# Sixteen small GpSimd loads into scratch tiles, beside a decode kernel that streams its cache

## The chip, the cores and the metric

The kernel runs on one core of a Trainium2 chip. The metric is device time in microseconds for one execution; the time before is the median of three runs, and one execution was also taken by the hardware profiler.

## What is computed

One decode step: attention over the last 4,096 positions of a cache and a dense block with the Mish activation, both on the same normalised input, added to the input.

```python
def _A_ref(x, k_cache, v_cache, wq, wo):       # x: 2 x 1 x 448, 16 query heads, 8 kv heads, 256 wide
    W = min(4096, max(256, Sk // 4))           # Sk = 32768: the last 4096 positions
    q = (x @ wq).reshape(B, Sq, Hq, Dh)...
    k, v = the last W rows of k_cache, v_cache, each kv head for two query heads
    p = _softmax(einsum("bhqd,bhkd->bhqk", q, k) * Dh ** -0.5)
    return einsum("bhqk,bhkd->bhqd", p, v)... @ wo
def _B_ref(x, w1, b1, w2):
    h = x @ w1 + b1
    return (h * tanh(softplus(h))) @ w2
xn = _layernorm(x)
return x + _A_ref(xn, ...) + _B_ref(xn, ...)
```

All inputs are bfloat16. The windows of both caches are 2 x 8 x 4096 x 256 values each, 33.6 MB for K and as much for V; with the weights 77.67 MB are read from HBM.

## The kernel before

The work on the caches is done in four turns, `u` = 0 to 3, each for two kv heads of both batch entries (`KU * Bsz` = 4 streams). A turn's keys come in two loads of 4 MB (`load_k`, L102), its values in two more (`load_v`, L110), and its slice of Wo in one (`load_wo`, L116). All of these are issued by SP, in program order, and go through a ring of three buffers of 4 MB, `kv_pool`; Wq, and at the end W2, take a buffer of the same ring. A load waits on SP until the buffer's last reader is done, and the loads written behind it wait too. W1 is loaded at L541, the ragged rows of W2 by `load_xb` and `load_xa` (L607, L613) in turns 0 and 1, and the rest of W2 at L638 after the loop. The only load of another queue is that of x (L123, on ACT).

In a turn, `turns` (L306) transposes a key buffer on VectorE, `scores` (L382 to L404) makes the scores on TensorE, their exponentials on ScalarE and transposes these on VectorE, `weigh` sums them, `values` (L439) multiplies with V, and `gather`, `finish`, `relay` and `mix_early` (L457 to L519) bring the result through Wo. In the last turn the second value buffer comes in three parts, of which the last two go through `values_fixed` (L472), and `mix` and `dense_out` (L286) end the sum. `pace` (L658) issues matmuls whose result is not used. The tile framework is under a manual schedule: each engine's instructions stand in the order in which the code is written, and semaphores are set where one engine's data is another's input or where a buffer is used again.

GpSimd (POOL) has set-up work only: constants, masks, zeroed tiles and four copies, the last of them the memset of `w2_x` at L537. Nothing in the loop is on GpSimd, and it issues no load. `consts` is a pool with one buffer for each tile, and tiles of the pool `small` are allocated after it. At the end of the program SP waits for every semaphore in use, and all engines go through closing barriers.

The loop around the change:

Of the kernel before, what the change touches and what calls it, by code (L numbers as in the profile page):

```python
# [11 lines left out]
BF16 = mybir.dt.bfloat16  # L12
FP32 = mybir.dt.float32
# [4 lines left out]
def kernel(  # L18
# [13 lines left out]
    nc = tc.nc  # L32
# [47 lines left out]
    consts = ctx.enter_context(tc.tile_pool(name="consts", bufs=1))  # L80
# [18 lines left out]
    def load_k(u, r):  # L99
        t = ring("k")  # L100
        src = kview[u][:, s0:, :].rearrange("j (c t) d -> c j (t d)", c=C)
        nc.sync.dma_start(out=t[:], in_=src[:, :, r * RK * KE : (r + 1) * RK * KE])  # L102
        k_t[u, r] = t

    def load_v(u, g, lo=0, hi=TV):
        if lo == 0:
            v_t[u, g] = ring("v")
        t = v_t[u, g]
        src = vview[u][:, s0:, :].rearrange("j (g x t) d -> g x j (t d)", g=GV, x=C)
        nc.sync.dma_start(  # L110
            out=t[:, lo * Dh : hi * Dh], in_=src[g, :, :, lo * Dh : hi * Dh]
        )

    def load_wo(u):
        w = wo_pool.tile([P, KU, rep, 2 * D], BF16, tag="wo", name="wo")
        nc.sync.dma_start(  # L116
            out=w[:].rearrange("p k h e -> p (k h e)"),
            in_=A_wo.rearrange("(k u y i) d -> u y k (i d)", k=KU, u=U, i=8)[u],
        )
        wo_t[u] = w  # L120
# [7 lines left out]
    for lo, hi in ((0, HW // 2), (HW // 2, NS * HW // 2), (NS * HW // 2, NS * HW)):  # L128
# [14 lines left out]
        out=halves[:], in_=ident[0:2, 0:2].unsqueeze(2).to_broadcast([2, 2, Bsz])  # L143
# [5 lines left out]
    for k in range(KU):  # L149
        nc.gpsimd.tensor_copy(  # L150
            out=hot[:, k, :, :, :, k],
            in_=ident[:].rearrange("p (q y) -> p y q", y=4).unsqueeze(2)
# [11 lines left out]
        out=rstd[:], in_=mv[:, 1:2], func=ACT.Sqrt, bias=eps_t[:], scale=1.0  # L164
# [4 lines left out]
        out=xn_bf[:],  # L169
# [8 lines left out]
        out=parm[:], in_=ident[:].rearrange("p (a o) -> p o a", o=2), axis=AXIS.X, op=ALU.add  # L178
# [3 lines left out]
        out=jm[:],  # L182
        in_=ident[:].rearrange("p (a j h) -> p j a h", j=J, h=rep),
# [4 lines left out]
        out=jm[:], in0=jm[:], scalar1=-1.0, scalar2=29952.0, op0=ALU.add, op1=ALU.mult  # L188
# [3 lines left out]
        out=mneg[:], in_=jm[:].unsqueeze(1).to_broadcast([P, TH * 8, J])  # L192
    )
    sel = consts.tile([P, 2, NQ], FP32)
    for x in range(2):
        for w in range(4):
            at = 32 * w + (2 * (w % 2) + x) * NQ
# [3 lines left out]
            else:  # L201
                nc.vector.tensor_tensor(
                    out=sel[:, x, :], in0=sel[:, x, :], in1=src, op=ALU.add
# [9 lines left out]
        out=pick_f[0:QB, 0:12],  # L213
        in_=idb.rearrange("p (a s) -> p a s", s=XB),
# [4 lines left out]
        out=pick_f[QB:P, XO:XP].rearrange("p (e r) -> p e r", r=4)[:, :, 0:2],  # L219
        in_=ida.rearrange("p (e r s) -> p e r s", r=2, s=XA),  # L220
# [4 lines left out]
        out=pick_f[QB:P, XP : XP + XA],  # L225
        in_=ida.rearrange("p (a s) -> p s a", s=XA),
# [4 lines left out]
        out=pick_f[0:QB, XP:],  # L231
        in_=idb.rearrange("p (a s) -> p s a", s=XB),
# [20 lines left out]
    for odd in range(2):  # L253
        for half in range(2):
            o = (half + odd) % 2
            nc.vector.tensor_scalar(
                out=xs[:, odd::2, half * Bsz : (half + 1) * Bsz],
# [45 lines left out]
    def turns(u, i):  # L303
        t = k_t.pop((u, i))
        for r in range(RK):
            nc.vector.transpose(  # L306
                out=kt[i][:, :, r, :, :],
                in_=t[:, r * KE : (r + 1) * KE].bitcast(FP32).rearrange(
                    "p (a c j) -> p a c j", c=P // (R * J), j=J
                ),  # L310
            )

    spread = {}
    for n in range(2):
        for e in range(2):
# [3 lines left out]
                out=sp[:],  # L319
                in_=ident[:, o : o + 63 : 2].unsqueeze(1).to_broadcast([P, G, 32]),  # L320
# [56 lines left out]
    def scores(u, i):  # L377
        if i == 0:
            state["ex"] = small.tile([P, T, 4, NH, J], BF16, tag="ex", name="ex", bufs=1)
        ex = state["ex"]  # L380
        sc = ps_sc.tile([P, T, 4, J], FP32, tag="sc", name="sc")
        nc.tensor.matmul(  # L382
            sc[:].rearrange("p t c m -> p (t c m)"),
            lhsT=ident[:],
            rhs=mneg[:].rearrange("p a j -> p (a j)"),
            start=True,
            stop=False,
            skip_group_check=True,
        )
        for n in range(NB):  # L390
            for e in range(2):
                for w in range(4):
                    nc.tensor.matmul(  # L393
                        sc[32 * w : 32 * (w + 1)].rearrange("p t c m -> p t (c m)"),
                        lhsT=qd[:, u, 2 * n + e, :, :].rearrange("p g q -> p (g q)"),
                        rhs=ktm[i][:, n, e, :, 16 * w : 16 * (w + 1)],
                        start=False,
                        stop=(n == NB - 1 and e == 1),
                        skip_group_check=True,
                    )  # L400
        nc.scalar.activation(out=ex[:, :, :, i, :], in_=sc[:], func=ACT.Exp, scale=scale)  # L401
        if i == NH - 1:
            for h in range(NH):
                nc.vector.transpose(  # L404
                    out=p_all[:, :, h * TH : (h + 1) * TH, :].rearrange("p g t q -> p t g q"),
                    in_=ex[:, h * TH : (h + 1) * TH].rearrange(
                        "p t c i m -> p t (c i m)"
                    ).rearrange("p t (g q) -> p t g q", g=G),
                )
            swap()  # L410
# [20 lines left out]
    def values(u, g, hi=TV):  # L431
        if g == 0:
            state["v", u] = ps_v.tile([P, 2, Dh], FP32, tag="v", name="pv")
        pv = state["v", u]
        v = v_t[u, g]
        for k in range(hi // 2):
            a, b = k // 2, k % 2
            w = 2 * (a % 2) + b
            nc.tensor.matmul(  # L439
                pv[32 * w : 32 * (w + 1), :, :].rearrange("p x d -> p (x d)"),  # L440
                lhsT=p_run[:, g, 4 * a : 4 * a + 4, :].rearrange("p t q -> p (t q)"),
                rhs=v[:, 2 * k * Dh : (2 * k + 2) * Dh],
                start=(g == 0 and a < 2),
                stop=(g == GV - 1 and a >= hi // 4 - 2),
                skip_group_check=True,
            )
# [92 lines left out]
    def load_w1():  # L539
        t = consts.tile([P, NS * F2], BF16, name="w1")  # L540
        nc.sync.dma_start(  # L541
            out=t[:], in_=B_w1.flatten().rearrange("(p e) -> p e", p=P)
        )
        state["w1"] = t
# [60 lines left out]
    def load_xb(r):  # L605
        rows = B_w2[F2 + FR : F2 + FR + QB, :].rearrange("(e r s) d -> r e (s d)", r=4, s=XB)
        nc.sync.dma_start(  # L607
            out=w2_x[r:12:4, :], in_=rows[r]
        )

    def load_xa(r):
        rows = B_w2[F2 + FR + QB :, :].rearrange("(e r s) d -> r e (s d)", r=2, s=XA)
        nc.sync.dma_start(out=w2_x[XO + r : XP : 4, 0 : XA * D], in_=rows[r])  # L613

    def dense_x():
        for s in range(XS):
            nc.tensor.matmul(  # L617
                early[:],
                lhsT=act_x[:, s, :],
                rhs=w2_x[:, s * D : (s + 1) * D],  # L620
                start=False,
                stop=False,
            )
# [19 lines left out]
    def dense_out(part):  # L643
        k, lo, hi = w2_parts[part]
        for i in range(lo, hi):
# [2 lines left out]
                act_bf[:, i, k, :], state["w2"][:, at : at + D], stop=(k == 1 and i == NR - 1)  # L648
            )

    load_w1()
    def pace(n, key=None):
        ps = ps_sc.tile([P, T, 4, J], FP32, tag="sc", name="pace")
        for i in range(n):
            rhs = mneg[:].rearrange("p a j -> p (a j)")
            if key is not None and i == 0:
                rhs = key
            nc.tensor.matmul(  # L658
                ps[:].rearrange("p t c m -> p (t c m)"),
                lhsT=ident[:],  # L660
                rhs=rhs,
                start=True,
                stop=True,
                skip_group_check=True,
            )
# [10 lines left out]
    for u in range(U - 1):  # L676
        load_k(u + 1, 0)
        load_v(u, 0)
        load_k(u + 1, 1)
        load_v(u, 1)  # L680
        load_wo(u)
        if u == 0:
            load_xb(0)
            load_xb(1)
            load_xa(0)
        if u == 1:
            load_xb(2)
            load_xb(3)
            load_xa(1)
        turns(u + 1, 0)  # L690
        values(u, 0)
        scores(u + 1, 0)
        turns(u + 1, 1)
        if u == U - 2:
            pace(11, key=ktm[1][:, 0, 0, :, 0:16])
        values(u, 1)
        gather(u)
        finish(u)
        scores(u + 1, 1)
        relay(u)  # L700
        if u == U - 2:
            dense_x()
        mix_early(u)
        if u < U - 2:
            weigh(u + 1)
    u = U - 1
# [67 lines left out]
```

## Time and profile before

| | us |
|---|---|
| median of 3 runs (lowest, highest) | 188.63 (188.61, 188.82) |
| profiled execution, its own time | 188.59 |
| its span | 186.8 |
| busy: PE / DVE / ACT / POOL | 88.9 / 97.1 / 12.6 / 7.8 |
| HBM read | 77.67 MB, 416 GB/s over the span |

The profiled execution's time is 1.8 us longer than its span, which goes from the first to the last instruction. Its time is 0.04 us under the median. TensorE's mean granted clock was 0.76. In the page, q1 is the queue of SP's loads, q10 that of ACT's, and q8 and q14 fetch instructions. Times inside the span count from its start.

### The profile page before, as it was taken

To read this page: it belongs to the slowest core of one execution; us is meant where nothing else is said; L and a number is where in the kernel's file an instruction comes from. 1 tells how busy PE (TensorE), PEld (TensorE's weight loads), DVE (VectorE), ACT (ScalarE), POOL (GpSimd) and SP (SyncE) were. 2 spreads that over 40 slices of the span, in tenths; PEclk is the share of its full clock that TensorE was granted. 3 is DMA by queue.
4 is the path that set the end of the run, shared out by engine and by line. 5 is a ranking of instruction groups with operands and counts; after the bars stand their busy time and mean duration, and the time that the engine had idled before them with its cause. 6 is when DMAs were issued, how large, how long until landed. Compare 5 with 4: busy or idle time off the path is not lost.

```text
span 186.8 us, 1974 instructions
## 1 busy us (share of the span) xinstructions
PE 88.9 (48%) x854; PEld 38.1 (20%) x854; DVE 97.1 (52%) x100; ACT 12.6 (7%) x27; POOL 7.8 (4%) x18
## 2 busy tenths in 40 slices
PE   0057015893209300783039101881059059899694
PEld 0022002541003100241013000330022013434353
DVE  6961798974792098028940296048920593040100
ACT  3004000101000100110000100110000000210100
POOL 8800000000000000000000000000000000000000
PEclk9999999955555855599555855798556756999999
DMA  6999999999999999999999999999999999999991
GB/s 207 442 475 442 407 435 405 452 446 444 414 421 421 432 449 389 472 442 442 414 435 418 449 435 401 468 446 407 421 435 428 442 449 421 449 389 430 403 406 73
DMA packets 4523, 77.78 MB, mean 416 GB/s; under 512 B 522, under 2 KB 912, under 8 KB 1956
## 3 DMA queue, kind: packets, MB, share of 16 engines
q1 hardware_dynamic: 4512, 77.67, 97.2%
q8 instruction: 6, 0.10, 0.2%
q14 instruction: 1, 0.01, 0.0%
q10 hardware_dynamic: 4, 0.00, 0.0%
HBM read 77.67 MB, written 0.00 MB: 416 GB/s over the span
## 4 chain that ended last, share of the span: by engine, by line
DMA 73%; DVE 12%; PE 9%; issue 3%; SPq 1%; ACT 0%
DMA k<-in_A_k_cache_dram 44%; DMA v<-in_A_v_cache_dram 29%; DVE kt L306 12%; PE pv L439 3%; PE acc L286 1%; PE sc L393 1%; PE early L519 1%; PE early L617 1%; PE o L472 1%; SPq L129 1%; PE pace L658 1%; PE o L457 1%; PE ox_ps L498 0%; SPq L102 0%; ACT vs L451 0%
## 5 line engine op out<-in xcount | busy, mean ns | idle before, releaser
L306 DVE STREAM_TRANSPOSE kt<-k 128x4096 f32<-128x4096 f32 x16 | 70.1, 4417 | 31.1 <-DMA k<-in_A_k_cache_dram 31.1
L439 PE MATMUL pv<-v,p 128*32 128x512 bf16 x244 | 23.2, 546 | 55.8 <-DMA v<-in_A_v_cache_dram 55.8
L393 PE MATMUL sc<-kt,qd 128*32 128x512 bf16 x256 | 22.6, 489 | 11.2 <-DVE kt L306 11.2
L439 PEld LDWEIGHTS <-p 128*32 128x32 bf16 x244 | 8.5, 124 | 68.4 <-issue 44.9
L658 PE MATMUL pace<-mneg,ident 128*128 128x512 bf16 x42 | 12.7, 440 | 0.0
L393 PEld LDWEIGHTS <-qd 128*32 128x32 bf16 x256 | 7.7, 114 | 24.1 <-issue 19.7
L484 DVE TENSOR_TENSOR oT<-o,rec 128x16 bf16<-128x16 f32 x4 | 0.7, 175 | 21.1 <-PE o L457 17.5
L404 DVE STREAM_TRANSPOSE p<-ex 128x512 bf16<-128x512 bf16 x8 | 5.2, 690 | 10.6 <-ACT ex L401 10.6
L401 ACT ACTIVATE ex<-sc 128x512 bf16<-128x512 f32 x8 | 4.8, 597 | 85.4 <-PE sc L393 85.4
L425 DVE TENSOR_REDUCE rec<-dn 128x8 f32<-128x512 f32 x4 | 2.8, 691 | 13.3 <-PE dn L417 13.3
L658 PEld LDWEIGHTS <-ident 128*128 128x128 bf16 x43 | 4.2, 111 | 13.7 <-DVE kt L306 7.8
L248 PE MATMUL xr_ps<-ident,xrows 2*128 2x2 bf16 x7 | 1.0, 182 | 11.2 <-DVE xrows L247 11.2
L451 ACT COPY vs<-pv 128x512 f32<-128x512 f32 x4 | 2.3, 586 | 54.0 <-PE pv L439 54.0
L519 PE MATMUL early<-wo,ox 128*2 128x448 bf16 x24 | 5.0, 352 | 1.3 <-ACT ox L510 1.3
L457 PE MATMUL o<-sel,vs 128*128 128x8 f32 x32 | 4.3, 262 | 2.1 <-ACT vs L451 2.1
L457 PEld LDWEIGHTS o<-sel,vs 128*128 128x128 f32 x32 | 4.2, 196 | 4.5 <-ACT vs L451 4.4
L417 PE MATMUL dn<-p,ones 128*128 128x512 bf16 x8 | 2.8, 438 | 3.8 <-DVE p L375 3.8
L382 PE MATMUL sc<-mneg,ident 128*128 128x512 bf16 x8 | 4.1, 516 | 0.0
L658 PE MATMUL pace<-kt,ident 128*128 128x512 bf16 x1 | 0.6, 609 | 7.3 <-DVE kt L306 7.3
L561 PE MATMUL h_ps<-xs,w 128*128 128x4 bf16 x49 | 3.3, 186 | 0.9 <-DMA w<-in_B_w_dram 0.9
L191 DVE CAST mneg<-jm 128x512 bf16<-128x512 f32 x1 | 3.5, 3481 | 0.0
L328 PE MATMUL q_ps<-wq,xs 128*32 128x512 bf16 x28 | 3.2, 627 | 0.4 <-issue 0.4
(85 smaller groups left out, 58.4 us busy)
## 6 DMA issues: line engine op xcount, KB each, us to landing
k<-in_A_k_cache_dram SPq DMA_DIRECT2D x8, 4096.0 KB, 26.4
v<-in_A_v_cache_dram SPq DMA_DIRECT2D x7, 4096.0 KB, 21.2
wo<-in_A_wo_dram SPq DMA_DIRECT2D x4, 896.0 KB, 21.5
v<-in_A_v_cache_dram SPq DMA_DIRECT2D x1, 2560.0 KB
wq<-in_A_wq_dram SPq DMA_DIRECT2D x1, 1792.0 KB, 10.2
w<-in_B_w_dram SPq DMA_DIRECT2D x1, 1568.0 KB
wq<-in_A_wq_dram SPq DMA_DIRECT2D x1, 1536.0 KB, 6.3
v<-in_A_v_cache_dram SPq DMA_DIRECT2D x1, 1024.0 KB
```

The costliest lines, as they stand in the source:

```text
L191: nc.vector.tensor_copy(out=mneg[:], in_=jm[:].unsqueeze(1).to_broadcast([P, TH * 8, J]))
L306: nc.vector.transpose(out=kt[i][:, :, r, :, :], in_=t[:, r * KE : (r + 1) * KE].bitcast(FP32).rearrange("p (a c j) -> p a c j", c=P // (R ...
L328: nc.tensor.matmul(q_ps[32 * u : 32 * (u + 1), :], lhsT=xs[:, s, :], rhs=wq_t[s][:, u * 512 : (u + 1) * 512], start=(s == 0), stop=(s == N ...
L382: nc.tensor.matmul(sc[:].rearrange("p t c m -> p (t c m)"), lhsT=ident[:], rhs=mneg[:].rearrange("p a j -> p (a j)"), start=True, stop=Fal ...
L393: nc.tensor.matmul(sc[32 * w : 32 * (w + 1)].rearrange("p t c m -> p t (c m)"), lhsT=qd[:, u, 2 * n + e, :, :].rearrange("p g q -> p (g q) ...
L401: nc.scalar.activation(out=ex[:, :, :, i, :], in_=sc[:], func=ACT.Exp, scale=scale)
L404: nc.vector.transpose(out=p_all[:, :, h * TH : (h + 1) * TH, :].rearrange("p g t q -> p t g q"), in_=ex[:, h * TH : (h + 1) * TH].rearrang ...
L439: nc.tensor.matmul(pv[32 * w : 32 * (w + 1), :, :].rearrange("p x d -> p (x d)"), lhsT=p_run[:, g, 4 * a : 4 * a + 4, :].rearrange("p t q ...
L457: nc.tensor.matmul(po[:, c, :], lhsT=sb[:, x, c::2], rhs=sel[:, x, :], start=(x == 0 and c == 0), stop=(last and x == 1), skip_group_check ...
L519: nc.tensor.matmul(early[:], lhsT=ox[:, i, :], rhs=w[:, i, :], start=False, stop=(u == U - 2 and i == 7),)
L561: nc.tensor.matmul(h_ps[:, i, :, :].rearrange("p k b -> p (k b)"), lhsT=w1_v[:, s, cols], rhs=xs[:, s, 0 : 2 * Bsz], start=False, stop=(s ...
L658: nc.tensor.matmul(ps[:].rearrange("p t c m -> p (t c m)"), lhsT=ident[:], rhs=rhs, start=True, stop=True, skip_group_check=True,)
```

## The change

Two scratch tiles are added to `consts`: `marks`, 32 partitions of 64 float32, and `marks_b`, 32 partitions of 96 bfloat16. Two helpers load the first rows of Wo into them with DMAs issued by GpSimd. `mark_cast(n, w)` loads `n` rows of `w` elements and widens them to float32; `mark_split(n, w)` loads `n` rows in two pieces of `w` elements each, in bfloat16. The calls stand in the loop over turns: seven in turn 0 and nine in turn 1, with `w` going up by two from 24 to 54. Each load takes rows of its tile that no other one takes. Nothing reads the tiles.

```diff
+    marks = consts.tile([32, 64], FP32)
+    marks_b = consts.tile([32, 96], BF16)
+    row_at = [0, 0]
+
+    def mark_cast(n, w):
+        at = row_at[0] % 28
+        row_at[0] += n
+        nc.gpsimd.dma_start(out=marks[at : at + n, 0:w], in_=A_wo[0:n, 0:w])
+
+    def mark_split(n, w):
+        at = row_at[1]
+        row_at[1] += n
+        nc.gpsimd.dma_start(
+            out=marks_b[at : at + n].rearrange("p (a e) -> p a e", a=2)[:, :, 0:w],
+            in_=A_wo[0:n, :].rearrange("p (a e) -> p a e", a=2)[:, :, 0:w],
+        )
+
     load_w1()
...
             load_xb(2)
             load_xb(3)
             load_xa(1)
+        if u == 0:
+            for i in range(7):
+                mark_cast(2, 24 + 2 * i)
+        if u == 1:
+            for i in range(3):
+                mark_split(2, 38 + 2 * i)
+            mark_cast(3, 44)
+            for i in range(4):
+                mark_cast(1, 46 + 2 * i)
+            mark_cast(5, 54)
         turns(u + 1, 0)
         values(u, 0)
```

## The prediction

> **What bounds the kernel now.** I read the page's slices first, then the chain that ended last, then a table by stage, then the queue table, and last the single packet records of the trace, since the change adds packets.
>
> The slices show a DMA row of nines from the second slice to the last but one:
>
> ```profile
> DMA  6999999999999999999999999999999999999991
> GB/s 207 442 475 442 407 435 405 452 446 444 414 421 421 432 449 389 472 442 442 414 435 418 449 435 401 468 446 407 421 435 428 442 449 421 449 389 430 403 406 73
> ```
>
> The chain says that the end is reached over landings of K and V, with little else in it:
>
> ```profile
> DMA 73%; DVE 12%; PE 9%; issue 3%; SPq 1%; ACT 0%
> ```
>
> The table by stage has the 16 DMA engines at a mean share of about 1.0 in every stage, whatever VectorE and TensorE do in it. (Columns: stage, its length, busy time of PE, PEld, DVE, ACT, POOL with instructions, granted clock, DMA share, GB/s.)
>
> ```profile
> 4.00:8.00 4.00, 0.00 (x0) 0.00 (x0) 3.89 (x6) 0.00 (x0) 4.00 (x8) 1.00 0.99 420
> 8.00:12.00 4.00, 0.79 (x6) 0.60 (x6) 3.74 (x22) 0.00 (x0) 0.41 (x1) 1.00 1.04 446
> 12.00:16.00 4.00, 3.63 (x31) 1.24 (x30) 0.61 (x4) 0.00 (x0) 0.00 (x0) 1.00 1.04 451
> 80.00:100.00 20.00, 8.57 (x87) 3.27 (x86) 11.87 (x10) 0.81 (x3) 0.00 (x0) 0.72 1.01 436
> 140.00:160.00 20.00, 11.74 (x93) 4.09 (x85) 8.77 (x2) 1.18 (x2) 0.00 (x0) 0.66 1.01 436
> ```
>
> In the packet records 1,920 packets of 32,768 B take 1,213 ns each, 27.0 B/ns, so 16 engines carry 432 GB/s; 77.67 MB at that rate are 179.7 us, and the stream runs from 1.75 us (first packet of Wq) to 183.73 (last of W2). It is never empty: the shortest time between an issue on SP and the first packet of that load, once the stream runs, is 5.9 us (V issued at 57.22, first packet at 63.13), elsewhere mostly 8 to 17. So compute has some 6 us of cover everywhere but in the tail, and **what takes time on a DMA engine comes out at the end one for one**. After the V landing at 179.15 the tail is fixed: TensorE to 184.4, the output's store, closing barriers to 186.8.
>
> **What the change adds.** Sixteen DMA issues on GpSimd's queue, with 26 widened rows and 6 rows in two pieces each: 38 runs of 48 to 108 B as read. They wait for nothing (the rows of the two scratch tiles do not overlap, nobody reads them), and GpSimd has nothing after its last memset:
>
> ```profile
> 5.33 3.08 POOL L537 MEMSET w_x<- 48x3584 bf16 x1
> ```
>
> So all sixteen go out from 8.41 us on, whatever turn of the loop they are written in. An issue from GpSimd is not in the trace; the nearest rows are the one on ACT's queue, 0.52 us, and those on SP's, 0.27 to 0.8. At 0.5 to 1 us each they are out by 16 to 24 us. Only the closing drain stands behind them on that queue, so the issue time is off the path.
>
> *VectorE beside GpSimd.* VectorE has been slow next to GpSimd's memsets: the cast at L191 took 3.48 us and ended just after the memset above, and a copy of 2x4 elements at L142 took 1.91. If issues from GpSimd hold VectorE's copies the same way, some twenty small copies and casts between 8.6 and 20.3 us are late, then the first key transposes (L306, from 21.50, after 1.21 us of idle). Even if VectorE stood still until 24 us the first V load would go out 3 to 6 us late, and it has 13.4 us in hand (issued 30.30, first packet 43.71). I cost it at nothing; the cover is the backlog, and a delay beyond 5.9 us that lasted to 57 us would come out whole.
>
> *The DMA engines.* This is the term that decides. By their bytes the marks are nothing: an 80 B packet took 9 ns, an 896 B one 41, a 4 B completion packet 9. But they come from a second queue, and the trace has seven packets on engines that were streaming for the first:
>
> ```profile
> q1 hardware_dynamic: 4512, 77.67, 97.2%
> q8 instruction: 6, 0.10, 0.2%
> q14 instruction: 1, 0.01, 0.0%
> ```
>
> In the packet records six of these were followed by a 32 KB packet of q1 that took far more than its 1,213 ns: after the instruction fetches at 39.16, 61.05, 100.64, 125.86 and 163.92 (16 KB each) 1,764, 1,707, 1,711, 1,713 and 1,681, and after the 8 KB one at 44.91, 1,745. The lengthening is 468 to 551 ns, mean 507, and does not grow with the size of the fetch. It isn't given back: from the start of the fetch at 163.92 to the end of the packet behind it are 2.62 us, where line rate for both would be 1.82. So an interlude from another queue costs its engine about 0.51 us besides its own packets. For a tiny packet it may be less, down to nothing; I have no row for that.
>
> [...]
>
> How many interludes does an engine get? The nearest row is the two-row load of x (q10): two data packets and two completion packets, so two engines touched. By that row 32 rows touch an engine 32 times in all, twice each if they go round the sixteen (the row counts 2x7, 2x3, 3, 1x4, 5 add up to 32, two laps). Twice 0.51, and two or three runs and their completions of up to 41 + 9 ns: 2 x 0.56 = 1.12 us. The bounds are 2 x 0.02 = 0.04 us (no loss at the change) and sixteen interludes on some engine, 16 x 0.56 = 9.0. I take 1.12, as the long packets are the only rows of a queue change and the load of x is the only small load.
>
> *The close.* At the end SP waits for the semaphores of all loads, two to an instruction, 64 ns apart (185.14, 185.20, ...), and then for the output, landed near 185.95. Up to eight further semaphores are four instructions, 0.26 us: nothing if they stand before the output's wait, which has 0.6 us to spare, 0.26 if behind. I take 0.1, with GpSimd's own closing drain (78 ns now) in it.
>
> The scratch tiles take 256 + 192 B of a partition and move the tiles allocated after them; no row prices an address, and I take 0.
>
> **Sum.** 1.12 + 0.1 = 1.2 us on the profiled execution's 188.59 us (186.8 of span), 189.8; the median of the runs, 188.63, is 0.04 higher, so 189.8 stands for both.
>
> **Rivals.**
> 1. *Tiny packets slip in for nothing.* The lengthening comes from the fetches' size or target, and the marks cost 16 x 9 ns of completions and three runs, 0.2 us, with 0 to 0.1 at the close: 188.7 to 188.9. For it: within q1 a completion packet costs nothing that shows, since an engine's sixteen packets of two K loads from 10.92 to 30.28 us take 1,210 ns each with a completion among them. Against it: those come from the same queue. The same time results if the loads turn out not to be made.
> 2. *Every mark touches every engine, or all touch the same few.* Sixteen interludes at 0.51 to 0.56 us: 8 to 9 us, 196.7 to 197.6. For it: the loads of W2's ragged rows (3 and 4 rows) leave only some engines late, so that the engines' spread grows from 0.5 us at 10.9 to 1.8 at 117. Against it: two marks waiting together cost one change. It decides once the interludes on the worst engine pass about eight. [...]
> 3. *Faster.* Each landing waits for the latest engine, and the spread at the last Wo load is 1.77 us (first packet 172.43, last end 176.38, against 8 x 272 ns). Each 16 KB fetch costs one engine about 1.4 us (2.62 - 1.21). If the new queue moves one fetch from a late engine to an early one, the latest engine gains what parts it from the next group, about 0.5 us: 188.1. It decides only if the marks themselves cost under that. Nothing shows that a fetch's engine depends on other queues.
>
> **How the numbers follow.** The forecast, an interlude cost paid a few times per engine (189.1 to 193), has 0.45; rival 1 has 0.26, rival 2 0.15, rival 3 0.14. The limit of 0.2%, 0.38 us, is about what a measurement of this kernel can tell from no change; forecast and rival 2 are beyond it, rival 1 inside, rival 3 beyond it on the other side. Faster 0.14, same 0.26, slower 0.60. The range takes in rivals 1 and 3 (188.1) and goes up to the point of eight interludes, 8 x 0.56 = 4.5, 193.0; rival 2 is left out. The likeliest case's own range is 189.1 to 193.0.
>
> **What would show it.** Right: a new software queue with packets between 8 and 25 us, 32 KB packets of q1 near 1,700 ns there and nowhere else new, two or so to an engine; the K landing that starts L306 at 21.50 about 1 us later, and the last V landing as late. Rival 1: no lengthened packets, the last V landing within 0.2 us of 179.15. Rival 2: the first K landing 5 us or more late. The forecast fails if the marks go out later than 25 us, if DMA's share falls under 0.9 in stages other than the early ones, or if the added time lies behind 184 us.

## The result and the profile after

The change made the kernel 0.5% slower: 189.55 us (median of 7 runs, 189.31 to 190.51) against 188.63 (7 runs, 188.52 to 188.90), a ratio of 1.0056 with a 95% interval of 1.0037 to 1.0074. The profiled execution took 189.87 us, 0.3 over its median, with a span of 187.7. The span was 186.8 us before and is 187.4 in the median of the runs, and the time outside the span went from some 1.8 us to 2.17. So about 0.6 us came inside the span and 0.36 outside it. One of the four executions of experiment e12 below, 196.83 us, was in a slow state, and its row goes by the other three.

The slices of the kernel after, as before, show a DMA row of nines (one slice has an eight):

```profile
DMA  6999999999999998999999999999999999999991
```

The queue table has the new queue. Its columns are packets, MB and share of 16 engines' time:

```profile
q1 hardware_dynamic: 4512, 77.67, 97.0%
q0 software_dynamic: 512, 0.01, 0.2%
```

It has 512 packets for sixteen loads, 32 a load. One load of two rows alone (experiment e2) shows two data packets and 30 of 4 B. The records don't name the engine, but in the kernel after sixteen of these packets start between 12.48 and 13.62 us, sixteen more between 13.70 and 14.83, and each in the second group some 1.22 us after one in the first: by that a load has two packets on each of the 16 engines.

GpSimd's timeline (start, length, engine, line, operation; the idle time before it and its releaser in brackets) shows the issues:

```profile
5.61 3.08 POOL L537 MEMSET w_x<- 48x3584 bf16 x1
8.64 3.72 POOL L658 DMA_DIRECT2D marks<-in_A_wo_dram  x7
12.35 0.60 POOL L663 DMA_DIRECT2D marks_b<-in_A_wo_dram  x1
15.47 0.58 POOL L663 DMA_DIRECT2D marks_b<-in_A_wo_dram  x1 [2.52 <-DMA marks<-in_A_wo_dram]
31.27 0.52 POOL L658 DMA_DIRECT2D marks<-in_A_wo_dram  x1 [1.91 <-DMA marks_b<-in_A_wo_dram]
```

Eight go out at once, 0.52 to 0.65 us each. From the ninth on each waits for the semaphore of the load eight places earlier, which it uses again: the ninth, at 15.47 us, names the first one's, whose last update came at 15.19, and the sixteenth, at 31.27, the eighth one's, at 30.99. Landing is slow on the full stream. The sixteen took 6.6 to 18.6 us, where the load of x, issued at 0.74 us before the stream ran, had its last packet at 1.70. Two groups in the list of DMA issues (KB, median us from issue to landing):

```profile
marks<-in_A_wo_dram POOLq DMA_DIRECT2D x2, 0.2 KB, 8.9
marks_b<-in_A_wo_dram POOLq DMA_DIRECT2D x1, 0.3 KB, 18.6
```

In the packet records the starts are those of engines that pass one packet of q0, then one of q1, then the next of q0: some 1.22 us after the first where q1's packets are of 32 KB, and sixteen starts in 0.47 to 0.49 us between 31.5 and 33.4 us, where they are of 12,544 B. The marks run from 12.5 to 43.5 us.

At the early end VectorE's first key transposes show how late the K loads landed; the first two lines are of before, the last two of after:

```profile
21.50 8.77 DVE L306 STREAM_TRANSPOSE kt<-k 128x4096 f32<-128x4096 f32 x2 [1.21 <-DMA k<-in_A_k_cache_dram]
31.18 8.77 DVE L306 STREAM_TRANSPOSE kt<-k 128x4096 f32<-128x4096 f32 x2 [0.90 <-DMA k<-in_A_k_cache_dram]
```
```profile
21.98 8.77 DVE L306 STREAM_TRANSPOSE kt<-k 128x4096 f32<-128x4096 f32 x2 [2.41 <-DMA k<-in_A_k_cache_dram]
31.52 8.77 DVE L306 STREAM_TRANSPOSE kt<-k 128x4096 f32<-128x4096 f32 x2 [0.77 <-DMA k<-in_A_k_cache_dram]
```

At the late end the chain that ended last, in order of time (start, us, what), has the last V landing that the tail waits for at 179.15 before and at 167.57 + 12.39 = 179.96 after, and from there the same tail. Before, then after:

```profile
166.78 12.37 DMA v<-in_A_v_cache_dram
179.20 0.96 PE o L472 x32
184.38 0.37 DVE res L740
```
```profile
167.57 12.39 DMA v<-in_A_v_cache_dram
180.01 0.96 PE o L472 x32
185.20 0.37 DVE res L767
```

So the first K landings are 0.3 to 0.5 us later, and the last V landing 0.8 in this execution. A single landing measures the stream only roughly (experiment e1, without a load, has the last V landing at 179.41, 0.26 us later than before); the bytes that q1 has moved measure it better. Counted from 8 us on and compared with the kernel before, the kernel after is only 0.11 us behind at 31 us (at 432 GB/s), 0.55 at 46, and 0.57 at 80, 100 and 160 us. Nearly all is lost while the marks run, 0.44 us of it between 31 and 46, and none is won back. With 0.07 us more in the close (below) that is the 0.6 us of the median span.

In the packet records the marks on the engines show in two parts. The 512 packets themselves took 0.35 us for each engine (5.59 us over 16). And 73 packets of q1 between 8 and 80 us took more than their usual time, against 7 before the change; the added time is 0.42 us an engine against 0.10. The new long ones last 1,227 to 1,535 ns in place of 1,213, most of them between 34 and 40 us. Together that is 0.35 + 0.32 = 0.67 us, more than the 0.57 that the stream lost, because a packet and the next one overlap. The starts show it: in e2 the 32 KB packet starts 5 to 6 ns after the small one, which takes 9 or 25; from one small packet to the next on its engine are 1,215 ns with no lengthening, where two 32 KB packets in a row start 1,209 to 1,210 ns apart. By that a completion costs its engine some 5 ns and not the 9 of its own record, an estimate.

### The profile page after: what moved, and what is told of

It reads as the page before. It is cut to its first block, busy times and chain, and to the rows that moved or that the text cites. A ratio compares the mean times of both kernels' runs of the same rounds, so it can differ in the third digit from the quotient of the medians.

```text
span 187.7 us, 1994 instructions
## 1 busy us (share of the span) xinstructions
PE 86.0 (46%) x854; PEld 37.6 (20%) x854; DVE 96.3 (51%) x100; ACT 12.6 (7%) x27; POOL 16.6 (9%) x34
## 4 chain that ended last, share of the span: by engine, by line
DMA 53%; DVE 24%; PE 18%; ACT 2%; SPq 1%; issue 1%
DMA v<-in_A_v_cache_dram 38%; DVE kt L306 18%; DMA k<-in_A_k_cache_dram 15%; PE pv L439 5%; PE sc L393 5%; DVE p L404 2%; PE o L457 2%; PE acc L286 1%; PE dn L417 1%; DVE rec L425 1%; ACT ex L401 1%; ACT vs L451 1%; PE early L519 1%; PE early L617 1%; PE o L472 1%
## 5 line engine op out<-in xcount | busy, mean ns | idle before, releaser
L439 PE MATMUL pv<-v,p 128*32 128x512 bf16 x244 | 22.5, 533 | 57.6 <-DMA v<-in_A_v_cache_dram 57.6
L393 PE MATMUL sc<-kt,qd 128*32 128x512 bf16 x256 | 20.8, 456 | 12.1 <-DVE kt L306 12.0
L658 POOL DMA_DIRECT2D marks<-in_A_wo_dram x13 | 6.9, 535 | 10.2 <-DMA marks<-in_A_wo_dram 8.2
```

Source lines behind the costliest of these rows:

```text
L393: nc.tensor.matmul(sc[32 * w : 32 * (w + 1)].rearrange("p t c m -> p t (c m)"), lhsT=qd[:, u, 2 * n + e, :, :].rearrange("p g q -> p (g q) ...
L439: nc.tensor.matmul(pv[32 * w : 32 * (w + 1), :, :].rearrange("p x d -> p (x d)"), lhsT=p_run[:, g, 4 * a : 4 * a + 4, :].rearrange("p t q ...
L658: nc.gpsimd.dma_start(out=marks[at : at + n, 0:w], in_=A_wo[0:n, 0:w])
```

## The experiments

The theories:

- **A**: any GpSimd load adds a fixed 0.36 us outside the span, and each load costs its two small packets on every engine, 0.02 to 0.03 us.
- **B**: all of the cost grows with the number of loads.
- **C** and **G**: the long q1 packets come from loads that are cut into runs of 12 to 20 B. In the list of instructions the loads of one row of 48, 50 and 52 are 16 runs of 3 elements, 10 of 5 and 13 of 4.
- **D**: the 0.36 us outside the span comes from the length of GpSimd's program. **E**: it comes from GpSimd's loads.
- **F** and **H**: any run, or any widened run, lengthens the stream's next packet by some 70 ns.
- The prediction's own: 0.5 us for an interlude.

All twelve, with the medians of the runs. The last two columns are from the packet records of the profiled execution. "Own" is the time of the q0 packets for each engine, and "longer" the time added to q1's packets between 8 and 80 us for each engine, less the 0.10 of before. "Behind" is how far q1's bytes since 8 us are behind those of the kernel before at 80 us; the kernel after has 0.57. The kernel before, run beside them: 188.67 to 188.68 us, span 186.8 to 186.85, outside 1.79 to 1.82.

| run | us | ratio (95%) | span | outside | own + longer | behind |
|---|---|---|---|---|---|---|
| e1 no loads | 188.79 | 1.0000 (0.9988 to 1.0012) | 187.0 | 1.79 | 0 | 0.00 |
| e2 one load | 188.72 | 1.0001 (0.9992 to 1.0010) | 186.9 | 1.80 | 0.02 + 0 | 0.02 |
| e3 sixteen equal | 189.25 | 1.0033 (1.0021 to 1.0045) | 187.15 | 2.15 | 0.32 + 0.03 | 0.22 |
| e4 thirty-two equal | 189.61 | 1.0050 (1.0038 to 1.0063) | 187.5 | 2.09 | 0.65 + 0.05 | 0.44 |
| e5 sixteen cut rows | 190.34 | 1.0090 (1.0076 to 1.0103) | 188.3 | 2.05 | 0.50 + 1.17 | 1.55 |
| e6 sixteen memsets | 188.65 | 0.9998 (0.9989 to 1.0007) | 186.8 | 1.81 | 0 | 0.02 |
| e7 eight equal | 189.12 | 1.0025 (1.0014 to 1.0037) | 187.2 | 2.07 | 0.16 + 0.01 | 0.11 |
| e8 sixteen, not widened | 189.30 | 1.0041 (1.0019 to 1.0063) | 187.2 | 2.10 | 0.29 + 0 | 0.19 |
| e9 256 runs of 64 B | 189.23 | 1.0034 (1.0024 to 1.0043) | 187.2 | 2.17 | 0.32 + 0.04 | 0.24 |
| e10 the same, widened | 189.23 | 1.0033 (1.0022 to 1.0043) | 187.15 | 2.04 | 0.56 + 0.25 | 0.45 |
| e11 256 runs of 12 B, rows apart | 189.36 | 1.0032 (1.0021 to 1.0044) | 187.35 | 1.98 | 0.50 + 0.20 | 0.37 |
| e12 128 runs of 1,536 B | 191.68 | 1.0157 (1.0140 to 1.0173) | 189.7 | 2.13 | 0.64 + 2.14 | 2.73 |

**How the cost grows (e1, e2, e7, e3, e4).** The calls in turns 0 and 1 are replaced; e1 has none, e2 one, e7 eight, e4 thirty-two with a tile of 64 rows:

```diff
-            for i in range(7):
-                mark_cast(2, 24 + 2 * i)
...
+            for i in range(16):      # e3
+                mark_cast(2, 32)
```

e1: 

> The two scratch tiles stay declared, all sixteen loads are left out. Every theory that puts the cost into the loads: 188.6 us (within 0.1 of before), time outside the span 1.8 us, no q0 packets. If moved addresses carried part of the cost: up to 0.3 us more.

e2: 

> One load (2 rows of 24, widened), the other fifteen left out. Theory A (a fixed price for any GpSimd load outside the span, 0.36 us, plus some 0.03 us per load for its two packets on each engine): 189.0, outside the span 2.15, q0 with 32 packets. Theory B (all of it grows with the number of loads): 188.7, outside the span 1.8. The prediction's own mechanism (0.5 us for each interlude on an engine): 188.6 to 189.1 and a lengthened 32 KB packet on two engines.

e3: 

> Sixteen loads all of 2 rows of 32, widened, in place of the sixteen lengths. Theory A: as after, 189.4 to 189.6, outside the span 2.15, 512 packets in q0. Theory C (the lengthened 32 KB packets after 34 us come from the one-row loads that are cut into runs of 12 to 20 B): 189.2, no group of 1.25 to 1.5 us packets in the stream. Prediction's mechanism: 189.8.

e4: 

> Thirty-two loads of 2 rows of 32, widened, into a tile of 64 rows. Theory A: 0.5 us over the sixteen equal ones, 189.9 to 190.1, outside the span 2.15, 1024 packets in q0. Theory B: twice the whole cost, 190.4, outside the span 2.5. If the cost is fixed and does not depend on the number: as sixteen, 189.3.

e7: 

> Eight loads of 2 rows of 32, widened. In the span 8 x 0.02 us over before for Theory A, 187.0. Outside: 1.8 if the number of waits or instructions sets it (the eight have no waits of their own), 2.15 if the eight semaphores do. So 188.8 or 189.15.

Tiles without loads cost nothing that shows in the time, and neither does one load. The stream shows the price of a load best: one, eight, sixteen and thirty-two loads put it 0.02, 0.11, 0.22 and 0.44 us behind, 0.014 us a load, well under the packets' own time. Inside the span theory A is right in kind, and its price is too high. The spans fit only roughly: from sixteen to thirty-two loads the median grows by 0.35 us (187.1 to 187.4 against 187.4 to 187.9), but eight loads have 187.2, where A expected 187.0, about as much as sixteen, and e1 without a load has 187.0. So the median of a few spans is good to some 0.2 us here. The page of e4 has the packets doubled:

```profile
q0 software_dynamic: 1024, 0.01, 0.3%
```

Outside the span A and B are both wrong in part: one load adds nothing, eight and sixteen add about 0.3, and thirty-two no more. The step lies between one and eight loads. Nor is it constant: of e7's twelve runs nine have 1.98 to 2.18 us outside the span and three 1.73 to 1.82, and one to three runs of e3, e8, e9, e10 and e12 have the short time too. The prediction's 0.5 us for an interlude is far off for small packets: one such for each load would be 8 us, and the sixteen loads, with two packets on every engine, put the stream 0.22 us behind.

**The cut rows (e5).**

```diff
+            for i in range(16):
+                mark_cast(1, 48)     # made into 16 runs of 3 elements by the program
```

> Sixteen loads all of 1 row of 48, widened, which the program makes into 16 runs of 3 elements each. Theory C (such runs lengthen the stream's packets, 0.1 us per load on each engine, from the long packets between 32 and 44 us in the changed kernel): 1.8 us over the sixteen equal two-row loads, 191.0. Theory A (only the number of loads and their two packets per engine count): 189.3 to 189.5, no group of long packets.

It is 1.1 us over the sixteen equal loads, less than the 1.8 expected but in C's direction. In the packet records 256 runs of 12 B lengthened q1's packets by 18.7 us in all, 73 ns a run, and the stream is 1.33 us further behind than with the equal loads. VectorE's second pair of transposes is later by more than a microsecond, and starts in two pieces:

```profile
22.32 8.77 DVE L306 STREAM_TRANSPOSE kt<-k 128x4096 f32<-128x4096 f32 x2 [3.00 <-DMA k<-in_A_k_cache_dram]
32.63 4.45 DVE L306 STREAM_TRANSPOSE kt<-k 128x4096 f32<-128x4096 f32 x1 [1.54 <-DMA k<-in_A_k_cache_dram]
```

The changed kernel has 39 such runs, in three of its loads; its long packets fall after 34 us, where those loads pass. It took 189.55 against 189.25 us for the sixteen equal ones, 0.30 us, and the packet records put 0.29 us more lengthening on its engines (0.32 against 0.03). The intervals of the two ratios overlap (1.0037 to 1.0074, 1.0021 to 1.0045), so the times alone leave this part likely. The stream shows it: 0.57 us behind against 0.22, and between 31 and 46 us, where the cut loads pass, 0.44 against 0.06. Its 39 runs lengthened q1's packets by some 0.12 us each, more than e5's 73 ns; why stays open.

**What about a run makes it dear (e8 to e11).** e8 makes the tile of e3 bfloat16. e9 to e11 load 16 rows instead of two, so that there are sixteen runs in each load, 256 in all:

```diff
+        to = marks[16 * (i % 8) : 16 * (i % 8) + 16, w * (i // 8) : w * (i // 8) + w]
+        nc.gpsimd.dma_start(out=to, in_=A_wo[16 * i : 16 * i + 16, 0:w])   # w = 32, 32, 3
```

e8: 

> Sixteen loads of 2 rows of 32 without widening (the tile is bfloat16). Theory A: as with widening, 189.25 (189.1 to 189.4). If widening costs on the engines: 0.1 to 0.3 us less.

e9: 

> Sixteen loads of 16 rows of 32, not widened: one run of 64 B for each engine and load, 256 in all, where the two-row loads have 32. Theory F (each run from the second queue lengthens the stream's next packet by some 70 ns, whatever it is): 1.1 us over the sixteen two-row loads, 190.3. Theory G (only runs of 12 to 20 B do): 189.3 to 189.4. Theory H (only widened runs of any length): 189.3 to 189.4.

e10: 

> The same sixteen loads of 16 rows of 32, widened to float32 (128 B written for each run). Theory F: 190.3. Theory G: 189.4. Theory H: 190.3 or more.

e11: 

> Sixteen loads of 16 rows of 3, widened: 256 runs of 12 B, as in e5, but each from and to a row of its own. Theories F, G and H: 190.3. If the cost in e5 comes from neighbouring runs of one row that are written by different engines: 189.3 to 189.4.

All four stay within 0.11 us of e3. Widening costs nothing that these times can tell (e8 against e3, e10 against e9). In the packet records it does cost a little: a 32 KB packet behind a widened run is some 15 ns longer (e3, e10), behind an unwidened run of 64 B not at all (e8, e9), and e10's stream is 0.21 us further behind than e9's. At 70 ns H falls, and F too, since 256 unwidened runs leave the stream nearly where 32 do, 0.24 us behind against 0.19. G as it was put falls as well: e11 has as many runs of 12 B as e5, and is 1 us faster. There a run lengthened q1's packets by only some 12 ns. What differs is that e5's runs are neighbours in one row, in the source and in the target; e11's have a row of their own on both sides. Which side matters was not tried. In e10 own and longer add up to 0.81 us, while the stream was 0.45 behind and the span grew by 0.35: packets overlap (the 5 to 6 ns from start to start in e2), so the two columns are not paid in full.

**A larger interlude (e12).**

```diff
+        nc.gpsimd.dma_start(out=marks[16 * i : 16 * i + 16, :], in_=A_wq[16 * i : 16 * i + 16, 0:768])
```

> Eight loads of 16 rows of 768, not widened: 128 runs of 1,536 B. By the eight small ones' 189.1 plus 128 x 57 ns / 16 = 0.46 us for the bytes at the stream's rate: 189.6. With 70 ns of lengthening for each run 0.56 us more, 190.1. If an interlude of a KB and more costs the prediction's 0.5 us: 8 x 0.5 = 4 us more, 193.5.

It lies between the expectations: 2.6 us over the eight small loads, where the bytes explain 0.46. Each run of 1,536 B lengthened q1's packets by 0.27 us (34.3 us over 128 runs), against 15 ns or less for the small runs of e8 to e11 and 0.5 us for the instruction fetches of 8 and 16 KB. By the starts of the packets about half of the 0.27 falls on the q1 packet behind the run and half on the one behind its completion, some 0.13 us each. The loss is there at the first K landings:

```profile
23.09 8.77 DVE L306 STREAM_TRANSPOSE kt<-k 128x4096 f32<-128x4096 f32 x2 [3.97 <-DMA k<-in_A_k_cache_dram]
34.09 4.45 DVE L306 STREAM_TRANSPOSE kt<-k 128x4096 f32<-128x4096 f32 x1 [2.22 <-DMA k<-in_A_k_cache_dram]
```

**Outside the span (e6, and all runs).**

```diff
+            for i in range(16):
+                nc.gpsimd.memset(marks[:, 4 * i : 4 * i + 4], 0.0)
```

> No loads; sixteen small memsets on GpSimd in their place. Theory D (the 0.35 us outside the span is an instruction fetch at the program's end, set by the length of GpSimd's program): 189.0, outside the span 2.15. Theory E (it comes from loads of GpSimd, their queue or semaphores): 188.65, outside the span 1.8.

Sixteen more instructions on GpSimd that are not loads leave the time outside the span at 1.81 us. So the number of GpSimd's instructions doesn't set it, and E is left of the two. The waits of the ninth and later loads don't set it either, since e7's eight loads have none and mostly took the longer time. Two rivals are not excluded: a load may be longer in the program than a memset, and eight loads also bring eight semaphores that SP waits for at the end (107 to 114 in the kernel after). In the packet records a sign goes with the longer time. In eight of the profiled executions (the changed kernel, e4, e5, e8 to e12) there is an instruction fetch of 8 KB on q14 some 1.8 to 2 us after the span's end, and all of these have 2.06 to 2.25 us outside the span. In the six others (before, e1, e2, e3, e6, e7) there is none, and they have 1.74 to 1.85. The profiled executions of e3 and e7 are among the few of theirs with the short time. So the 0.3 us and a late fetch go together, in programs with eight or more GpSimd loads. Why such a program has that fetch, and whether it is the cause, stays open.

## Why the prediction was right, and where its steps were not

The time fell inside the range and moved the way that was forecast, by 0.92 us where 1.2 was expected. What held is the bound: time lost on the DMA engines came out at the end. That the sum came near is in good part luck: its two factors were off in opposite directions, and more than a third of the measured time lies outside the span, where no term stood. By the prediction's own signs its mechanism didn't hold either. Between 8 and 33 us the longest 32 KB packet of q1 took 1,228 ns, not near 1,700, and the marks ran past 25 us.

- *The bound.* Right. DMA's share was 0.98 to 1.11 by stage from 4 to 180 us, and what the stream lost it didn't win back: 0.57 us behind became 0.6 us of span, and the 2.73 of e12 became 2.9.
- *Interludes on an engine.* The number was mis-sized: two were taken from the load of x, and there were 32 packets, two for each of the sixteen loads. Rival 2 was right that every mark touches every engine. The argument against it, that two marks waiting together cost one change, was an assumption that no row of before showed, and it doesn't hold: even the two packets of one load stand 1.22 us apart on their engine, with a 32 KB packet between them (e2).
- *The price of one.* Mis-sized the other way: 0.56 us each was carried over from the fetches of 8 and 16 KB, because between those two the lengthening did not grow. By the runs it does grow below that: 15 ns or less for runs of 12 to 128 B with rows of their own, some 130 a packet in e12. So 2 x 0.56 = 1.12 us stood for a loss of 0.57: 0.22 as for sixteen equal loads (e3), and 0.35 more, the most of it from the three cut loads, which the prediction took as ordinary rows.
- *Rival 1* had the price of the packets right, 0.2 us against the 0.22 of e3. Its 188.7 to 188.9 misses the cut rows and the time outside the span.
- *When they go out.* Wrong: until 31.8 us, not 24, by the wait of each load for the one eight before. Their packets ran to 43.5. The sign named for failure, marks out later than 25 us, did appear. That the issues were late cost nothing, as nothing but the close is behind them on GpSimd.
- *VectorE beside GpSimd.* Costed at nothing, and right, for a simpler reason than the backlog: the casts at L236 and L237 took 0.17 us each, and the seven copies at L247 1.02, the same as before, while GpSimd was issuing.
- *The close.* 0.1 us, measured 0.07: from the output's issue to the end of the span are 2.05 us against 1.98, with GpSimd's closing drain and clear longer by 28 and 43 ns. The waits for the eight new semaphores (185.96 to 186.39 us) stand before the output's, at 186.78.
- *Outside the span.* Taken as unchanged; it grew by 0.36 us. The sum was made against the execution's own time, but no term was asked for that lies outside.
- *The scratch tiles* cost nothing that can be told (e1, 0.9988 to 1.0012).
- *Rivals 2 and 3.* No engine lost anything near 8 us, and nothing was gained.

## What to carry to other kernels

In this kernel, whose DMA share was 0.98 to 1.11 by stage from 4 to 180 us, each load took its price from the stream, small, early and unread as it was: 0.014 us for a two-row load from GpSimd, which has 32 packets (e2 to e4), and 0.3 us for one with sixteen runs of 1,536 B (e12). To see such a price, compare the bytes that the stream has moved by the same time; it tells 0.1 us where spans and landings scatter by 0.2 and more. Don't carry a price over from rows a hundred times larger: the change of queue that cost 0.5 us behind 8 KB cost 0.015 or less behind 128 B (e10). Ask for the time outside the span as well, and look at how a load is cut: one row of 48 elements became sixteen runs of 3.

## What was not expected of the hardware

Small GpSimd loads beside a full stream took 6.6 to 18.6 us to land, as their packets went through one at a time on an engine, 1.22 us apart with a 32 KB packet of the other queue between, and the semaphores' reuse then held GpSimd's own issues until 31.27 us. Neighbouring runs of 12 B from one row lengthened the stream's packets by 73 ns a run (e5), runs of 12 B with rows of their own by some 12 (e11). And programs with eight or more such loads mostly took 0.2 to 0.4 us longer outside the span; the profiled executions that did have an instruction fetch after the program's end, the others none.
